# Mixer products in strips of the TensorE array: four strips of 32 columns, then four of 32 rows

## The chip, the core and the metric

The kernel runs on one core of a Trainium2 chip. Its engines work in parallel, each through its own list of instructions in order: TensorE (PE; its weight loads are listed as PEld), VectorE (DVE), ScalarE (ACT), GpSimd (POOL), and SyncE (SP), which here only issues DMAs. They wait for one another through semaphores. TensorE writes its products to PSUM, eight banks of 512 fp32 columns on 128 partitions; the other data lies in SBUF. The metric is the device time of one execution in microseconds.

## The reference

First attention with normalised queries and keys, over 8 batches, 12 heads, 448 positions and 64 dimensions a head; its output, the heads side by side, is a row of 768 for each position. Then a mixer over the positions, of rank 32, and an MLP.

```python
q_n, k_n = rmsnorm(q, g_q), rmsnorm(k, g_k)
attn = softmax(q_n @ k_n.T / 8)          # per batch and head: 448 x 448
x = (attn @ v)                           # per batch, heads side by side: 448 x 768
h = x.T @ U @ V                          # U: 448 x 32, V: 32 x 448
u = x + h.T
out = u + relu(u @ w_ch1) @ w_ch2        # 768 -> 3072 -> 768
```

## The kernel before

Positions are laid on the 128 partitions, three full blocks and a rest of 64, and two neighbouring batches share the block that holds their rests. `xs[b]` holds the attention output of batch b as `[128, 4, 768]` in bf16, `uT` the mixed rows turned (768 on the partitions in six tiles), which is what the first product of the MLP reads. Below, b counts from 0: batch 2 of the title is b = 1.

**The two lists.** After the attention of b = 0, the work stands in two lists. `att` holds the attention of the later batches: `Spair` (the scores of a pair of heads: two products into single banks of the pool `ps`, four into two double-bank tiles of the pool `ps_sc`, one more into `ps`, all but the last on 64 rows of the array, and five exponentials on ACT), `V` (14 products with the values, then a reciprocal and a multiplication on VectorE), and the preparation of the next queries and keys (squares on ACT, sums on VectorE, roots on ACT, scaling on GpSimd, `turn_dma` with four transposing DMAs on SP, `take_dma` with two multiplications on GpSimd). `mlp` holds `up` (six products of 448 columns and a relu), `down` (six products of 384 columns; four of these parts make a tile, which VectorE adds to u and SP stores), and the mixers of b = 1 to 7.

**The planner.** The loop that begins at line 884 takes from one list or the other. It carries `at`, its own estimate of when TensorE, ACT and VectorE will be free, from the costs that each step declares with `runs`; `due` says how far attention should be for a given progress of the MLP, and `ready` holds back scores where ACT or VectorE is late by these estimates. It fixes an order; on the chip each engine follows its own part of it.

**The pools.** `ps` has four banks, `ps_sc` two tiles of two banks, which together are all eight. A tile of a pool is given again when its last reader is done.

**The mixer of b = 1 to 7** is placed among the last steps of `down` of the batch before (line 770: 14 steps before their end for b = 1, 20 for the others):

- `mix_t` (line 480): the first product, x times U, turned. For each of six column tiles of x, four products with the x tile as weights and U, 32 columns, as the moving side: 24 products. VectorE copies the result, 128 x 192, into one of two buffers.
- `mix_tr` (line 491): two transposes on TensorE, which bring the rank onto the partitions (32 of them for each of four column tiles), and a copy on VectorE.
- `mix_rows` (line 530), eight times, for each of four blocks of rows and each half of 384 columns: three products with `Vm` as weights, 128 columns each. `Vm` holds V four times, each copy in its own 32 partitions with zeros in the others, so that a product over all 128 rows picks one column tile. VectorE adds x (line 546). After the second half SP issues one transposing DMA into `uT` (line 552), four a batch. The first `up` of the batch reads `uT` and needs all four.

One step of `down` stands between two of these parts. Where scores come in between, the parts are moved back by a step (lines 909 to 915). `turning` keeps loads back until the last part. The mixer of b = 0 uses another path (`mix_t0`, `mix` and `mix_rows` with `tz`), which stays.

Of the kernel before, what the change touches and what calls it, by code (L numbers as in the profile page):

```python
# [13 lines left out]
ALU = AluOpType  # L14
# [12 lines left out]
def kernel(  # L27
# [278 lines left out]

    NQ = P // rank
    Vf = outp.tile([P, dm], FP32, name="ob", tag="ob")[:, :S]
    Vm = consts.tile([P, NQ, S + R], BF16)

    nc.gpsimd.memset(Vm, 0.0)

    def prep_v(lo, hi):
        for m in range(lo, hi):
            r = slice(m * rank, (m + 1) * rank)
            cols = Vf[r].rearrange("r (p j) -> r j p", j=NT)
            nc.gpsimd.tensor_copy(Vm[r, m, :SM].rearrange("r (t i p) -> r i t p", i=2, t=NJ),
                                  cols[:, :2 * NJ].rearrange("r (i t) p -> r i t p", i=2))
            nc.gpsimd.tensor_copy(Vm[r, m, SM:S], cols[:, 2 * NJ])


    Uz = first[:, 0, :NW * P].rearrange("p (j r) -> p j r", r=P)
# [3 lines left out]
        nc.gpsimd.tensor_copy(Ub, Uf)  # L326
        nc.gpsimd.tensor_copy(Uz[:, :, :rank], Uf[:, :NW, :])

    tb_bufs = [consts.tile([P, 2 * P], BF16, name=f"tb{i}") for i in range(2)]

    def fill_mixer():
        nc.gpsimd.memset(Uz, 0.0)
        for t in tb_bufs:
            nc.gpsimd.memset(t, 0.0)


    at = {"pe": 0.0, "act": 0.0, "dve": 0.0}
# [2 lines left out]
    def runs(eng, us):  # L340
        at[eng] = us + (at["pe"] if eng == "pe" else max(at["pe"], at[eng]))
# [137 lines left out]

    def mix_t(b):  # L480

        pt = ps.tile([P, KD, rank], FP32, name="pu", tag="ps")
        for dt in range(KD):
            for j in range(NW):
                nc.tensor.matmul(pt[:, dt, :], xs[b][:, j, dt * P:(dt + 1) * P], Ub[:, j if j < NJ else NJ + b % 2, :],  # L485
                                 start=(j == 0), stop=(j == NW - 1))
        nc.vector.tensor_copy(tb_bufs[b % 2][:, :KD * rank], pt.rearrange("p k r -> p (k r)"))
        runs("pe", 0.62)
        runs("dve", 0.35)

    def mix_tr(b):
        pt = ps.tile([P, 2, P], BF16, name="pw", tag="ps")
        for i in range(2):
            nc.tensor.transpose(pt[:, i, :], tb_bufs[b % 2][:, i * P:(i + 1) * P], ident)
        tTs[b] = headp.tile([P, 2, P], BF16, name="tT", tag="tT")
        nc.vector.tensor_copy(tTs[b], pt)
        runs("pe", 0.11)
        runs("dve", 0.3)

    def mix_t0(lo, hi, scalar=False):  # L500

# [8 lines left out]
    def mix(b, dt, scalar=False):  # L510
        off = 64 if b % 2 == 0 else 0
        ph = ps.tile([P, S], FP32, name="ph", tag="ps")
        xb = xs[b][:, :, dt * P:(dt + 1) * P]
        nc.tensor.matmul(ph, tz[:, dt * P:(dt + 1) * P], Vm[:, 0, :S], start=True, stop=False)
# [15 lines left out]
    def mix_rows(b, w, half):  # L530

        odd = b % 2
        off = 0 if odd else 64
# [3 lines left out]
        if b < ROWS_FROM:  # L537
            nc.tensor.matmul(ph, Vm[:, 0, vc:vc + P], tz[:, h], start=True, stop=True)
        for i in range(HALF // P) if b >= ROWS_FROM else ():
            dt = half * (HALF // P) + i  # L540
            nc.tensor.matmul(ph[:, i * P:(i + 1) * P], Vm[:, dt % NQ, vc:vc + P], tTs[b][:, dt // NQ, :],  # L541
                             start=True, stop=True)
# [3 lines left out]
        nc.vector.tensor_tensor(dst, ph[lo:hi], x[lo:hi], ALU.add)  # L546
        runs("pe", 0.17)
        runs("dve", 0.56)
        if half == 1 and b >= ROWS_FROM:
            full = xs[b][:, w, :] if w < NJ else u_rest[lo:hi, :]  # L550
            c = off + w * P
            nc.sync.dma_start_transpose(uT[:, :, c:c + hi - lo], full)

    def up(b, ht):
        off = 64 if b % 2 == 0 else 0
# [92 lines left out]
    def turns(gi):  # L648
# [16 lines left out]
        (3, 1): [V2(2, 0)],  # L665
        (3, 2): turns(2),
        (3, 3): [V2(2, 1), (0, take_k, (2, 1)), (0, squares, (3, 0, pool)), (0, values, (2,)), (0, load, (5,)),
                 (0, weights, (1,)), (0, prep_v, (0, 1)), (0, squares, (3, 1, pool)), (0, weights, (1,))],
# [5 lines left out]
        (5, 3): [(0.39, mix, (0, 1)), (0.2, mix_t0, (512, 640)), (0, prep_v, (1, NQ)), (0, weights, (2,))],  # L674
    }
    for i in range(NPAIR):
        for r in range(4):
# [89 lines left out]
            done_at[a[0]] = n + 1 if a[0] > 0 else first_done  # L767


    PRE = (14, 20)  # L770
    mlp = []
    for b in range(B):
        for ht in range(KH):
# [5 lines left out]
        nb = b + 1  # L779
        pre = {}  # L780
        if ROWS_FROM <= nb < B:
            pre[n - PRE[nb > 1]] = [(0.77, mix_t, (nb,), nb)]
            pre[n - PRE[nb > 1] + 1] = [(0.11, mix_tr, (nb,), nb)]
            for piece in range(2 * NW):
                pre.setdefault(n - PRE[nb > 1] + 2 + (piece if nb > 1 else piece // 2), []).append(
                    (0.17, mix_rows, (nb, *divmod(piece, 2)), nb))
        tiles = [(col, half) for col in cols for half in range(2)]
        if b == 0:
            tiles.sort(key=lambda t: t[1])
# [73 lines left out]
        return a_two + (a_all - a_two) * (c - SECOND) / (m_end - m_one - SECOND)  # L863

    def mixes(f):
        return f in (mix_t, mix_tr, mix_rows)

    def ready(f, a):
        if f is Spair:
            if im > 0 and mixes(mlp[im - 1][1]):  # L870
                return False
            return at["dve"] <= at["pe"] + 0.3 and at["act"] <= at["pe"] + 1.0
        if f is V and ca >= a_one and (after_pair or after_v):
            return False
        if f is sums and a[0] > DMA_FROM:
            return not any(m[1] in (mix_t, mix_tr) for m in mlp[max(0, im - 1):im + 3])
        if ca >= a_one:
            return True
        if f is V:
            return exp_done[a[:2]] <= at["pe"] + 0.1  # L880
        return f is not Srows or at["act"] <= at["pe"] + 0.6

    later, turning, after_pair, after_v = [], False, False, False
    while ia < len(att) or im < len(mlp):
# [21 lines left out]
            if f is T and a == (DMA_FROM - 1, 1):  # L906
                nc.vector.memset(kp[:, 2 * NJ:], 0.0)
        else:
            if after_pair and mixes(mlp[im][1]):
                nb, n, moved = mlp[im][3], im, []  # L910
                while mixes(mlp[n][1]) and mlp[n][3] == nb:
                    e = next(i for i in range(n, len(mlp)) if mlp[i][1] is down)
                    moved += [mlp[e], *mlp[n:e]]
                    n = e + 1
                mlp[im:n] = moved
            after_pair = after_v = False
            c, f, a, _ = mlp[im]
            f(*a)
            turning = f is mix_t and a[0] > 0 or turning and a != (a[0], NW - 1, 1)
            cm += c  # L920
            im += 1

# [29 lines left out]
```

## Time and profile before

| | |
|---|---|
| median of 3 runs | 582.67 us (581.82 to 583.47) |
| profiled execution | 582.16 us, span 580.3 us |
| PE, PEld | 570.9 us (98%), 338.7 us (58%) |
| ACT | 308.2 us (53%) |
| POOL | 210.2 us (36%) |
| DVE | 196.3 us (34%) |
| granted TensorE clock | 1.00 |

The span is what the instructions of the core cover; the time also holds what lies around it. A product on TensorE is listed with its duration to the last result, but the next may start long before that, so the cost of a product in a stream is read from differences of starts, not from its own duration. A form such as 64*128 beside a product tells how many rows and columns of the array it uses.

### The profile page before, as it was taken

What the parts mean: (1) busy time and instruction counts of PE and PEld (TensorE: products, weight loads), DVE (VectorE), ACT (ScalarE), POOL (GpSimd) and SP (SyncE); (2) the same over time, 40 slices, a digit from 0 to 9 for tenths busy, and PEclk for the clock granted to TensorE, in tenths of its full rate; (3) what the DMA queues carried; (4) which work ended last, traced back from release to release, by engine and by line L of the source; (5) the groups of instructions that cost most, each with busy time, mean ns of one, the idle gap of its engine ahead of it and who ended that gap; (6) DMA issues with size and microseconds to landing.
All of it is one profiled execution on the core that took longest, in us unless ns stands there. A gap on an engine that the chain in (4) does not pass through costs nothing.

```text
span 580.3 us, 11778 instructions
## 1 busy us (share of the span) xinstructions
PE 570.9 (98%) x4850; PEld 338.7 (58%) x4850; DVE 196.3 (34%) x459; ACT 308.2 (53%) x510; POOL 210.2 (36%) x310
## 2 busy tenths in 40 slices
PE   8899999999999999999999999999999999999997
PEld 7655556555665556655566555665556555655565
DVE  5676656212353232521244230542034210410011
ACT  6866660787445776277635568357752444014300
POOL 5995684265314514334514532441531000000000
PEclk9999999999999999999999999999999999999999
DMA  9899999683547642765247745366204210330022
GB/s 235 168 241 241 244 232 223 128 209 73 135 79 170 156 106 35 175 179 130 36 123 116 179 104 122 80 159 150 36 16 102 49 28 1 54 76 1 1 55 55
DMA packets 104829, 68.21 MB, mean 118 GB/s; under 512 B 66632, under 2 KB 101704, under 8 KB 104776
## 3 DMA queue, kind: packets, MB, share of 16 engines
q1 hardware_dynamic: 95124, 57.83, 43.2%
q0 software_dynamic: 9408, 9.44, 9.7%
q8 instruction: 38, 0.62, 0.5%
q10 hardware_dynamic: 244, 0.20, 0.1%
q14 instruction: 15, 0.12, 0.1%
HBM read 52.20 MB, written 11.01 MB: 109 GB/s over the span
## 4 chain that ended last, share of the span: by engine, by line
PE 92%; ACT 2%; DMA 1%; POOL 1%; DVE 1%; issue 1%; SPq 0%; POOLq 0%; ACTq 0%
PE ph L558 36%; PE po L605 36%; PE pv L466 6%; PE sc L436 2%; PE pv L462 2%; PE sl L427 2%; PE sl L438 2%; PE pm L541 2%; PE po L592 1%; ACT E L416 1%; PE sc L415 1%; DMA qT<-qn 1%; PE pu L485 1%; DMA qf<-in_q_dram 1%; PE pt L354 1%
## 5 line engine op out<-in xcount | busy, mean ns | idle before, releaser
L605 PE MATMUL po<-w2b,hT 128*128 128x384 bf16 x1296 | 229.6, 326 | 0.0
L558 PE MATMUL ph<-uT,w1b 128*128 128x448 bf16 x1140 | 228.7, 352 | 0.0
L605 PEld LDWEIGHTS <-hT 128*128 128x128 bf16 x1296 | 122.1, 98 | 71.8
L558 PEld LDWEIGHTS <-w1b 128*128 128x128 bf16 x1140 | 108.3, 98 | 93.7 <-issue 0.7
L565 ACT ACTIVATE hT<-ph 128x448 bf16<-128x448 f32 x184 | 98.2, 551 | 116.6 <-PE ph L558 115.2
L429 ACT ACTIVATE E<-sl,gg 128x448 bf16<-128x448 f32 x72 | 41.6, 630 | 71.7 <-PE sl L427 71.7
L193 POOL TENSOR_TENSOR qn<-qf,rs 128x384 bf16<-128x384 f32 x36 | 29.9, 830 | 137.5 <-ACT rs L170 126.8
L386 POOL TENSOR_SCALAR qT<-qT,gg 128x448 bf16<-128x448 bf16 x36 | 50.5, 1403 | 73.6 <-DMA qT<-qn 63.5
L469 DVE RECIPROCAL r<-pv 128x4 f32<-128x4 f32 x96 | 17.5, 182 | 173.0 <-PE pv L466 172.8
L441 ACT ACTIVATE E<-sc,gg 128x896 bf16<-128x896 f32 x72 | 69.0, 1024 | 0.0
L615 DVE TENSOR_TENSOR ob<-po,x 128x384 f32<-128x384 f32 x46 | 25.7, 558 | 99.8 <-PE po L605 97.6
L466 PE MATMUL pv<-va,E 128*128 128x65 bf16 x1152 | 57.1, 194 | 0.0
L466 PEld LDWEIGHTS <-E 128*128 128x128 bf16 x1152 | 50.5, 98 | 6.3
L162 DVE TENSOR_REDUCE ssq<-sq 128x14 f32<-128x896 f32 x45 | 46.8, 1078 | 2.4 <-ACT sq L140 2.3
L462 PE MATMUL pv<-vl,E 128*128 128x130 bf16 x192 | 42.2, 220 | 0.3 <-ACT E L416 0.2
L470 DVE TENSOR_TENSOR x<-pv,r 128x256 bf16<-128x256 f32 x96 | 40.7, 424 | 3.3
L416 ACT ACTIVATE E<-sc,gg 128x896 bf16<-128x896 f32 (+1 forms) x42 | 37.5, 951 | 3.5 <-PE sc L415 3.3
L546 DVE TENSOR_TENSOR x<-pm,x 128x384 bf16<-128x384 f32 x48 | 26.1, 552 | 11.3 <-PE pm L541 9.1
L193 POOL TENSOR_TENSOR kp<-kf,rs 128x384 bf16<-128x384 f32 x36 | 29.9, 830 | 0.0
L169 ACT ACTIVATE rs<-ssq,eps 128x28 f32<-128x28 f32 (+1 forms) x25 | 7.9, 314 | 38.0 <-DVE ssq L162 33.7
L462 PEld LDWEIGHTS <-E 128*128 128x128 bf16 x192 | 18.7, 97 | 9.7 <-issue 2.0
L439 ACT ACTIVATE E<-sl,gg 128x448 bf16<-128x448 f32 x36 | 23.0, 638 | 0.0
(105 smaller groups left out, 401.0 us busy)
## 6 DMA issues: line engine op xcount, KB each, us to landing
qf<-in_q_dram SPq DMA_DIRECT2D x23, 448.0 KB, 3.8
kf<-in_k_dram SPq DMA_DIRECT2D x23, 448.0 KB, 5.3
vf<-in_v_dram SPq DMA_DIRECT2D x48, 192.0 KB, 5.3
out_dram<-ob SPq DMA_DIRECT2D x48, 192.0 KB, 2.8
w1b<-in_moe_w_ch_dram POOLq DMA_DIRECT2D x4, 1152.0 KB, 19.8
w2b<-in_moe_w_ch_dram POOLq DMA_DIRECT2D x8, 576.0 KB, 18.0
vf<-in_v_dram SPq DMA_DIRECT2D x48, 32.0 KB, 5.1
out_dram<-ob SPq DMA_DIRECT2D x13, 96.0 KB, 3.4
```

The lines of the kernel that those rows point to most:

```text
L162: nc.vector.tensor_reduce(ssqs[gi][:, i, :], sqs.pop((gi, i)), AX, ALU.add)
L193: nc.gpsimd.tensor_tensor(main.rearrange("p (t i) d -> p i t d", i=2), src[:, c, :2 * NJ].rearrange("p (i t) d -> p i t d", i=2), rs[:, c, ...
L386: nc.gpsimd.tensor_scalar(qT[:, a], qT[:, a], gg[:, 0:1], None, ALU.mult)
L416: nc.scalar.activation(es[(b, pr)][:, 2 * r:2 * r + n, :], sc[:, :n, :S], AF.Exp, scale=scal, bias=bias)
L429: nc.scalar.activation(E[:, 4 + i, :], ts[i], AF.Exp, scale=scal, bias=bias)
L441: nc.scalar.activation(E[:, 2 * r:2 * r + 2, :], tiles[r][:, :, :S], AF.Exp, scale=scal, bias=bias)
L462: nc.tensor.matmul(pv[:, i].rearrange("p e d -> p (e d)"), E[:, 2 * NJ, w:w + P], vl[:, lp, :], start=True, stop=False)
L466: nc.tensor.matmul(pv[:, i, e, :], E[:, 2 * j + e, w:w + P], va[:, (first_h + step * e) * NJ + j, :], start=False, stop=(e == 1 and j == N ...
L470: nc.vector.tensor_tensor(xs[b].rearrange("p i (h d) -> p i h d", d=D)[:, 2 * half:2 * half + 2, h0:h0 + step + 1:step, :], pv[:, :, :, :D ...
L558: nc.tensor.matmul(ph, w1b[:, dt, ht * P:(ht + 1) * P], uT[:, dt, off:off + S], start=(dt == 0), stop=(dt == KD - 1))
L565: nc.scalar.activation(hT[:, ht, off:off + S], ph, AF.Relu)
L605: nc.tensor.matmul(po, hT[:, ht, col:col + P], w2b[:, ht, half * HALF:(half + 1) * HALF], start=(ht == 0), stop=(ht == KH - 1))
```

## The change

The mixers of b = 1 to 7 use parts of the array.

- The first product takes U as the weights, 32 columns of the array, and x as the moving side, 192 columns. Four such products, one for each quarter of the 768 columns of x, go to four strips of 32 array columns and write four groups of 32 partitions of one bank. With four blocks of positions these are 16 products. The result has the rank on the partitions already, so the two transposes and their copy go.
- The second product takes 32 partitions of V as weights and the matching 32 partitions of the result as the moving side, on a strip of 32 array rows: for a block of rows, four products of 192 columns, one for each strip, into four different banks. `mix_two` does this for two blocks at once: eight products into both tiles of `ps_sc`, the banks that scores use, and then four additions on VectorE and two transposing DMAs. A mixer has two of them.
- `Vr`, V four times over the partitions without the zeros, takes the place of `Vm`; b = 0 reads it too, its other rows meeting zeros in `tz`. GpSimd fills and copies less.
- In the planner, `mix_two` stands 2 and 5 (b = 1) or 2 and 6 steps of `down` behind `mix_t`; where scores have just been placed, or ACT or VectorE is late by the planner's estimate, one step of `down` is taken first. `ready` and `turning` are fitted to the new names.

```diff
-    Vm = consts.tile([P, NQ, S + R], BF16)
-    nc.gpsimd.memset(Vm, 0.0)
-    def prep_v(lo, hi):
-        for m in range(lo, hi):
...
+    QC = dm // NQ
+    Vr = consts.tile([P, S + R], BF16)
+    nc.gpsimd.memset(Vr[:, S:], 0.0)
+    def prep_v():
+        cols = Vf.rearrange("r (p j) -> r j p", j=NT)
+        nc.gpsimd.tensor_copy(Vr[:, :SM].rearrange("r (t i p) -> r i t p", i=2, t=NJ),
+                              cols[:, :2 * NJ].rearrange("r (i t) p -> r i t p", i=2))
+        nc.gpsimd.tensor_copy(Vr[:, SM:S], cols[:, 2 * NJ])
...
     def mix_t(b):
-        pt = ps.tile([P, KD, rank], FP32, name="pu", tag="ps")
-        for dt in range(KD):
-            for j in range(NW):
-                nc.tensor.matmul(pt[:, dt, :], xs[b][:, j, dt * P:(dt + 1) * P], Ub[:, j if j < NJ else NJ + b % 2, :],
-                                 start=(j == 0), stop=(j == NW - 1))
-        nc.vector.tensor_copy(tb_bufs[b % 2][:, :KD * rank], pt.rearrange("p k r -> p (k r)"))
-        runs("pe", 0.62)
+        pt = ps.tile([P, QC], FP32, name="pu", tag="ps")
+        for j in range(NW):
+            for g in range(NQ):
+                nc.tensor.matmul(pt[g * rank:(g + 1) * rank, :], Ub[:, j if j < NJ else NJ + b % 2, :],
+                                 xs[b][:, j, g * QC:(g + 1) * QC], start=(j == 0), stop=(j == NW - 1))
+        tTs[b] = headp.tile([P, QC], BF16, name="tT", tag="tT")
+        nc.vector.tensor_copy(tTs[b], pt)
+        runs("pe", 0.6)
         runs("dve", 0.35)
-    def mix_tr(b):
...
+    def mix_two(b, ws):
+        odd = b % 2
+        off = 0 if odd else 64
+        ts = [ps_sc.tile([P, 2, 512], FP32, name="sc", tag="sc") for _ in range(2)]
+        for i, w in enumerate(ws):
+            vc = w * P if w < NJ else (SM if odd else S - P)
+            for g in range(NQ):
+                r = slice(g * rank, (g + 1) * rank)
+                nc.tensor.matmul(ts[g // 2][:, g % 2, i * QC:(i + 1) * QC], Vr[r, vc:vc + P], tTs[b][r], start=True, stop=True)
+        runs("pe", 0.4)
+        for i, w in enumerate(ws):
+            lo, hi = (0, P) if w < NJ else (0, R) if odd else (R, P)
+            full = xs[b][:, w, :] if w < NJ else u_rest[lo:hi, :]
+            for half in range(2):
+                h = slice(half * HALF, (half + 1) * HALF)
+                nc.vector.tensor_tensor(full[:, h].rearrange("p (g c) -> p g c", g=2),
+                                        ts[half][lo:hi, :, i * QC:(i + 1) * QC],
+                                        xs[b][lo:hi, w, h].rearrange("p (g c) -> p g c", g=2), ALU.add)
+                runs("dve", 0.56)
+            c = off + w * P
+            nc.sync.dma_start_transpose(uT[:, :, c:c + hi - lo], full)
...
-    PRE = (14, 20)
+    PRE, GAP = (14, 20), (5, 6)
...
-            pre[n - PRE[nb > 1]] = [(0.77, mix_t, (nb,), nb)]
-            pre[n - PRE[nb > 1] + 1] = [(0.11, mix_tr, (nb,), nb)]
-            for piece in range(2 * NW):
-                pre.setdefault(n - PRE[nb > 1] + 2 + (piece if nb > 1 else piece // 2), []).append(
-                    (0.17, mix_rows, (nb, *divmod(piece, 2)), nb))
+            at_ = n - PRE[nb > 1]
+            pre[at_] = [(0.6, mix_t, (nb,), nb)]
+            pre[at_ + 2] = [(0.4, mix_two, (nb, (0, 1)), nb)]
+            pre[at_ + GAP[nb > 1]] = [(0.4, mix_two, (nb, (2, 3)), nb)]
...
-            return not any(m[1] in (mix_t, mix_tr) for m in mlp[max(0, im - 1):im + 3])
+            return not any(m[1] is mix_t for m in mlp[max(0, im - 1):im + 3])
...
-            if after_pair and mixes(mlp[im][1]):
...
+            f = mlp[im][1]
+            if after_pair and mixes(f) or f is mix_two and max(at["act"], at["dve"]) > at["pe"]:
+                e = next((i for i in range(im, len(mlp)) if mlp[i][1] is down), None)
+                if e is not None and mlp[e][3] < mlp[im][3]:
+                    mlp.insert(im, mlp.pop(e))
...
-            turning = f is mix_t and a[0] > 0 or turning and a != (a[0], NW - 1, 1)
+            turning = f is mix_t or turning and not (f is mix_two and a[1][1] == NW - 1)
```

More of the change, by code (lines that the diff above doesn't have):

```diff
@@ L308 @@
     Vf = outp.tile([P, dm], FP32, name="ob", tag="ob")[:, :S]
-    Vm = consts.tile([P, NQ, S + R], BF16)
-    nc.gpsimd.memset(Vm, 0.0)
-    def prep_v(lo, hi):
-        for m in range(lo, hi):
[L315 to L319, printed above, removed]
+    QC = dm // NQ
+    assert NQ == 4 and 2 * QC <= 512 and HALF == 2 * QC
+    Vr = consts.tile([P, S + R], BF16)
[5 more added lines that the diff above has]
+        nc.gpsimd.tensor_copy(Vr[:, SM:S], cols[:, 2 * NJ])
     Uz = first[:, 0, :NW * P].rearrange("p (j r) -> p j r", r=P)
@@ L327, in prep_u @@
         nc.gpsimd.tensor_copy(Uz[:, :, :rank], Uf[:, :NW, :])
-    tb_bufs = [consts.tile([P, 2 * P], BF16, name=f"tb{i}") for i in range(2)]
     def fill_mixer():
         nc.gpsimd.memset(Uz, 0.0)
-        for t in tb_bufs:
-            nc.gpsimd.memset(t, 0.0)
     at = {"pe": 0.0, "act": 0.0, "dve": 0.0}
@@ L480, in mix_t @@
     def mix_t(b):
-        pt = ps.tile([P, KD, rank], FP32, name="pu", tag="ps")
-        for dt in range(KD):
-            for j in range(NW):
-                nc.tensor.matmul(pt[:, dt, :], xs[b][:, j, dt * P:(dt + 1) * P], Ub[:, j if j < NJ else NJ + b % 2, :],
-                                 start=(j == 0), stop=(j == NW - 1))
-        nc.vector.tensor_copy(tb_bufs[b % 2][:, :KD * rank], pt.rearrange("p k r -> p (k r)"))
-        runs("pe", 0.62)
-        runs("dve", 0.35)
-    def mix_tr(b):
[L492 to L498, printed above, removed]
+        pt = ps.tile([P, QC], FP32, name="pu", tag="ps")
@@ L513, in mix @@
         xb = xs[b][:, :, dt * P:(dt + 1) * P]
-        nc.tensor.matmul(ph, tz[:, dt * P:(dt + 1) * P], Vm[:, 0, :S], start=True, stop=False)
+        nc.tensor.matmul(ph, tz[:, dt * P:(dt + 1) * P], Vr[:, :S], start=True, stop=False)
         for j in range(NJ):
@@ L532, in mix_rows @@
         odd = b % 2
-        off = 0 if odd else 64
         h = slice(half * HALF, (half + 1) * HALF)
@@ L536, in mix_rows @@
         vc = w * P if w < NJ else (SM if odd else S - P)
[L537 to L542, printed above, removed]
+        nc.tensor.matmul(ph, Vr[:, vc:vc + P], tz[:, h], start=True, stop=True)
         x = xs[b][:, w, h]
@@ L548, in mix_rows @@
         runs("dve", 0.56)
[L549 to L552, printed above, removed]
     def up(b, ht):
@@ L667 @@
         (3, 3): [V2(2, 1), (0, take_k, (2, 1)), (0, squares, (3, 0, pool)), (0, values, (2,)), (0, load, (5,)),
-                 (0, weights, (1,)), (0, prep_v, (0, 1)), (0, squares, (3, 1, pool)), (0, weights, (1,))],
+                 (0, weights, (1,)), (0, prep_v, ()), (0, squares, (3, 1, pool)), (0, weights, (1,))],
         (4, 0): [V2(3, 0)],
@@ L673 @@
         (5, 2): [V2(4, 1), (0.39, mix, (0, 0))],
-        (5, 3): [(0.39, mix, (0, 1)), (0.2, mix_t0, (512, 640)), (0, prep_v, (1, NQ)), (0, weights, (2,))],
+        (5, 3): [(0.39, mix, (0, 1)), (0.2, mix_t0, (512, 640)), (0, weights, (2,))],
     }
@@ L865, in mixes @@
     def mixes(f):
-        return f in (mix_t, mix_tr, mix_rows)
+        return f in (mix_t, mix_two)
     def ready(f, a):
@@ L908 @@
         else:
-            if after_pair and mixes(mlp[im][1]):
[L910 to L915, printed above, removed]
+            f = mlp[im][1]
[3 more added lines that the diff above has]
+                    mlp.insert(im, mlp.pop(e))
             after_pair = after_v = False
```

## The prediction

> **What bounds the kernel now.** I read the page first (engines, chain), then a table of busy time in three stretches, then the timeline around one mixer (the mixing of a batch's rows through U and V) with no attention near it and around one with attention, and last the groups and DMA issues that the changed steps touch.
>
> The page's engines and its chain by engine, then the three stretches (busy us and instructions of each engine):
>
> ```profile
> PE 570.9 (98%) x4850; PEld 338.7 (58%) x4850; DVE 196.3 (34%) x459; ACT 308.2 (53%) x510; POOL 210.2 (36%) x310
> ...
> PE 92%; ACT 2%; DMA 1%; POOL 1%; DVE 1%; issue 1%; SPq 0%; POOLq 0%; ACTq 0%
> ```
>
> ```profile
> 0.00:45.00 45.00, 39.41 (x499) 28.85 (x500) 29.65 (x89) 32.45 (x50) 37.51 (x55) 1.00 0.97 215
> 45.00:465.00 420.00, 419.59 (x3614) 244.33 (x3613) 151.39 (x337) 249.73 (x413) 172.68 (x256) 1.00 0.59 130
> 465.00:580.00 115.00, 111.86 (x744) 65.48 (x740) 15.31 (x33) 26.00 (x48) 0.00 (x0) 1.00 0.16 34
> ```
>
> TensorE (PE) is busy 419.59 of the middle 420 us, at a granted clock of 1.00. All seven changed mixers lie after 45 us. There the time is the sum of what TensorE must issue: a microsecond off its list is a microsecond off the kernel, if no new wait appears.
>
> The mixer of batch 8 on TensorE (start, duration to the last result, line, count):
>
> ```profile
> 496.64 0.76 PE L485 MATMUL pu<-Ub,x 128*128 128x32 bf16 x24
> 497.25 1.14 PE L605 MATMUL po<-w2b,hT 128*128 128x384 bf16 x6
> 498.22 0.28 PE L494 MATMUL pw<-ident,tb 128*128 128x128 bf16 x2
> 498.33 1.14 PE L605 MATMUL po<-w2b,hT 128*128 128x384 bf16 x6
> 499.31 0.33 PE L541 MATMUL pm<-tT,Vm 128*128 128x128 bf16 x3
> 499.47 1.14 PE L605 MATMUL po<-w2b,hT 128*128 128x384 bf16 x6
> ```
>
> Differences of starts are the cost in the stream: 24 products of 32 columns take 0.61 us (25 ns each), two transposes 0.11, three products of 128 columns 0.16 to 0.17 (56 ns each), six of 384 columns 0.975 (163 ns each).
>
> Attention in the same stretch, all engines, rows left out:
>
> ```profile
> 225.04 1.14 PE L605 MATMUL po<-w2b,hT 128*128 128x384 bf16 x6
> ...
> 226.10 0.36 PE L427 MATMUL sl<-qT,kT 64*128 64x448 bf16 x2
> ...
> 226.30 0.54 PE L436 MATMUL sc<-qT,kT 64*128 64x448 bf16 x4
> ...
> 226.78 0.36 PE L438 MATMUL sl<-qT,kT 128*128 128x448 bf16 x1
> ...
> 226.98 1.14 PE L605 MATMUL po<-w2b,hT 128*128 128x384 bf16 x6
> ...
> 228.07 1.92 ACT L441 ACTIVATE E<-sc,gg 128x896 bf16<-128x896 f32 x2
> ```
>
> The 64*128 rows use half of the array's rows each; two of them together last 0.36 us, as long as one, so they run side by side. The whole set of scores takes 226.02 (225.04 + 0.975) to 226.98, 0.96 us, for four slots of 448 columns at 0.189 (six up products take 1.135) = 0.76. The other 0.20 is one change into the split array and back. The last exponential, which frees the score banks, ends at 229.99, 3.0 us after the scores.
>
> Groups and DMA issues that the changed steps touch:
>
> ```profile
> L546 DVE TENSOR_TENSOR x<-pm,x 128x384 bf16<-128x384 f32 x48 | 26.1, 552 | 11.3 <-PE pm L541 9.1 <-PE pm L538 2.2
> L496 DVE COPY tT<-pw 128x256 bf16<-128x256 bf16 x7 | 2.0, 292 | 9.1 <-PE pw L494 9.1
> ```
>
> ```profile
> uT<-x SPq DMA_TRANSPOSE x21, 2.8
> uT<-u_rest SPq DMA_TRANSPOSE x7, 2.4
> ```
>
> **The change part by part**, for one of seven batches.
>
> Removed from TensorE: 0.61 (first product) + 0.11 (transposes) + 8 x 0.167 = 1.33 (second product) = 2.05 us.
>
> Added, first product: 16 products of 192 columns in strips of 32 array columns. Between the 56 ns at 128 columns and the 163 at 384, 192 columns cost 83 ns. The trace has no strips of array columns. Ends: four strips side by side, 4 x 0.083 + 0.20 = 0.53; one after another, 16 x 0.083 + 0.20 = 1.52. I take side by side, since the 64*128 pairs are the nearest row, but with each weight load and product starting no closer than the 25 ns of the first product's row, the closest that any row shows for pairs of load and product in the full array: 16 x 0.025 + 0.20 = 0.60.
>
> Added, second product: twice eight products of 192 columns in strips of 32 rows. Ends: 2 x 0.083 + 0.20 = 0.37 each, or 8 x 0.083 + 0.20 = 0.86 each. By the same choice 8 x 0.025 + 0.20 = 0.40, together 0.80. The row tiling of the scores is the same mechanism with two strips, so I trust this more.
>
> Sum: 1.40 against 2.05, 0.65 a batch, 4.55 us in seven. Ends: 0.79 a batch (5.5 us) with all side by side at 83 ns a step, and a loss of 1.19 a batch (8.3 us) with nothing side by side.
>
> A rule speaks against the strips of columns. The Trainium skill (TensorE: Matmul & The Clock Gate, Part 3, "What overlaps and what doesn't") says that a weight load overlaps a running product only where their row groups differ; strips of columns share all rows. By that rule the first product would pay loads and products in turn. The trace disagrees for the whole array: 24 loads on the same rows last 96 ns each, yet start 25 ns apart; for strips of columns no run here shows it. By that rule the sum comes to the second price of the first rival below, 587.8; by the row, to 578.6.
>
> VectorE: the copy after the transposes (0.29 us) goes; the eight additions of 0.55 stay, now in two runs of four. The first copy stays at 0.36. VectorE is busy 36% of the middle stretch and hides this. GpSimd loses a 1.8 us fill, two of 0.3 and 3.5 us of copies of V, all before 45 us, where the chain to the first up products does not pass through them: nothing. SP issues the same four transposes a batch (1.2 us each), but in two bursts behind two runs of additions.
>
> New waits, by the order in the changed program. (a) A half mixer takes all four score banks, so it waits for the exponentials 3.0 us after the scores. In batches 3, 4 and 5 one half mixer stands exactly three steps of down (2.93 us) behind scores: 0.15 us each; the others stand further. TensorE runs in order, so everything behind waits too. (b) The next scores need the banks back from VectorE: from the half mixer's start 0.4 us to the first addition (before, a second product at 229.04 is followed by its addition at 229.41), 4 x 0.55, so 2.6, or 3.2 when a step's own addition is queued ahead. In batch 2 scores follow two steps of down later and reach the banks at about 2.7: 0.4 us. (c) Others that I can't place: some 0.1 us in each of the later batches. Taken together 1.0 us; bounds 0 and, from every half mixer waiting for one more pair of square activations that ACT has in front (0.97 each, 0.33 us a half on average), 4.6.
>
> Profiled execution 582.16 us (span 580.3 and 1.9 around it), less 4.55, plus 1.0: 578.6. It stood 0.5 below the median of the runs, 582.67, as near as these repeat.
>
> **The rivals.**
>
> Strips of columns one after another. For it: no row shows them working. Against: row strips do. Price: 1.52 instead of 0.60, 0.92 x 7 = 6.4 us, which gives 585.0; where loads are also not hidden (16 x 0.025 more a batch), 587.8. It decides as soon as the first product takes over 1.1 us.
>
> The banks eat the gain. For it: four banks, all taken, with ACT busy 59% of the middle stretch; against: most half mixers stand 3.4 us or more behind scores. With 4.6 us of waits the time is 582.2, no change.
>
> The transposes come late, and the first up product of each batch stalls: the mechanism that could make it slower with the products as cheap as I say. Place: the second half mixer's end. Before, eight additions came one by one over eight steps. Now the last additions end 2.6 to 3.2 us after the half mixer starts, the last transpose issues at 2.8 to 3.3 and lands 2.4 later (4.8 at the slowest of the 28): 5.2 to 8.1 us. Cover, from the order: 7.2 us in batch 3 (six steps of down 5.85, two value products 0.96, itself 0.40), 8 to 9.6 in batches 2 and 4 to 7, over 13 in batch 8. It costs from 7.2 on; if SP holds the transposes for 2 us more, behind the transposes of q and k that wait for GpSimd, six batches lose some 1.9 each: 11.4 us, 590.
>
> **How the numbers follow.** Strips side by side with small waits 0.66: 576.7 (5.5 saved, no wait) to 580.4. Gain eaten 0.13, around 582.2. Columns in turn 0.10, 585.0 to 587.8. Transposes late 0.11, around 590. A measurement here tells 0.3% (1.75 us) from no change: the first case is faster, the second the same, the last two slower. Range 576.5 to 585.0, which leaves out the late transposes and most of the columns in turn; the likeliest case's own range is 576.7 to 580.4.
>
> **What would show it.** Right: 16 first products with a form 128*32, four of them starting within 0.1 us, and the next down step 0.55 to 0.65 us after the first of them; eight second products in about 0.4; the middle stretch still nearly without gaps on TensorE. Wrong: starts 83 ns apart in the first product; a wait of TensorE on the exponential at the half mixers or on VectorE at the scores; a gap before the first up product of a batch that ends with the landing of a transpose.

## The result

The changed kernel takes 577.32 us (median of four executions, 577.21 to 579.24) against 582.32 us for the kernel before beside it: a ratio of 0.9919 with a 95% interval of 0.9906 to 0.9932, that is 4.7 us less by the ratio and 5.0 by the medians. A second set on another occasion gave 577.55 against 581.85, 0.9924 (0.9912 to 0.9937). The forecast was 578.6, with a range of 576.5 to 585.0. One execution of the runs below, the profiled one of the kernel with its first product on the whole array, fell into a slower state (600.56 us at a granted clock of 0.948, its nine others 583.1 to 584.5) and is left out.

The profiled execution took 577.21 us, with a span of 575.3 (before: 582.16 and 580.3).

### The profile page after: what moved, and what is told of

It reads as the page before. It is cut to its first block, busy times and chain, and to the rows that moved or that the text cites. A ratio compares the mean times of both kernels' runs of the same rounds, so it can differ in the third digit from the quotient of the medians.

```text
span 575.3 us, 11525 instructions
## 1 busy us (share of the span) xinstructions
PE 565.6 (98%) x4723; PEld 326.0 (57%) x4724; DVE 194.2 (34%) x452; ACT 307.3 (53%) x510; POOL 205.3 (36%) x302
## 4 chain that ended last, share of the span: by engine, by line
PE 93%; DMA 2%; ACT 2%; POOL 1%; issue 1%; DVE 1%; SPq 0%; POOLq 0%; ACTq 0%
PE ph L558 38%; PE po L605 36%; PE pv L461 6%; PE sc L431 2%; PE pv L457 2%; PE sl L422 2%; PE sl L433 2%; PE po L592 1%; DMA qf<-in_q_dram 1%; PE sc L410 1%; DMA vf<-in_v_dram 1%; ACT E L411 1%; PE sc L496 1%; PE pt L349 1%; POOL kp L174 1%
## 5 line engine op out<-in xcount | busy, mean ns | idle before, releaser
L605 PE MATMUL po<-w2b,hT 128*128 128x384 bf16 x1296 | 223.8, 326 | 0.0
L503 DVE TENSOR_TENSOR x<-sc,x 128x384 bf16<-128x384 f32 x42 | 20.8, 551 | 15.7 <-PE sc L496 15.7
L457 PEld LDWEIGHTS <-E 128*128 128x128 bf16 x192 | 18.7, 97 | 10.4 <-issue 2.7
```

Source lines behind the costliest of these rows:

```text
L457: nc.tensor.matmul(pv[:, i].rearrange("p e d -> p (e d)"), E[:, 2 * NJ, w:w + P], vl[:, lp, :], start=True, stop=False)
L605: nc.tensor.matmul(po, hT[:, ht, col:col + P], w2b[:, ht, half * HALF:(half + 1) * HALF], start=(ht == 0), stop=(ht == KH - 1))
```

## The profile after

The page's engines and its chain by engine:

```profile
PE 565.6 (98%) x4723; PEld 326.0 (57%) x4724; DVE 194.2 (34%) x452; ACT 307.3 (53%) x510; POOL 205.3 (36%) x302
...
PE 93%; DMA 2%; ACT 2%; POOL 1%; issue 1%; DVE 1%; SPq 0%; POOLq 0%; ACTq 0%
```

The three stretches (length, then busy us and instructions of PE, PEld, DVE, ACT, POOL, the granted clock, DMA share, GB/s):

```profile
0.00:45.00 45.00, 39.38 (x504) 28.76 (x506) 30.79 (x89) 32.55 (x51) 33.58 (x47) 1.00 0.98 216
45.00:465.00 420.00, 419.31 (x3540) 236.10 (x3538) 150.06 (x335) 250.23 (x415) 171.76 (x256) 1.00 0.61 131
465.00:575.00 110.00, 106.92 (x685) 61.19 (x682) 13.34 (x28) 24.49 (x45) 0.00 (x0) 1.00 0.15 32
```

TensorE is still busy all through the middle stretch (419.31 of 420, before 419.59) at a clock of 1.00, and still makes the chain. The time fell because its list is shorter: 565.6 us busy instead of 570.9.

The mixer of batch 8 in the timeline, where no attention is near (start, duration to the last result, line, form, count):

```profile
492.53 0.51 PE L480 MATMUL pu<-x,Ub 128*32 128x192 bf16 x16
492.98 2.12 PE L605 MATMUL po<-w2b,hT 128*128 128x384 bf16 x12
495.03 0.34 PE L496 MATMUL sc<-tT,Vr 32*128 32x192 bf16 x8
495.31 4.07 PE L605 MATMUL po<-w2b,hT 128*128 128x384 bf16 x24
499.31 0.34 PE L496 MATMUL sc<-tT,Vr 32*128 32x192 bf16 x8
499.59 5.70 PE L605 MATMUL po<-w2b,hT 128*128 128x384 bf16 x34
```

The form `128*32` is the strip of 32 columns, `32*128` the strip of 32 rows. Differences of starts hide a part here, because the change of form delays the first product itself: the last `down` product is followed by the first product after 256 to 259 ns instead of 162. With that included (from the start of the last product before, plus its own 162 ns, to the start of the next `down` product), the single records of the trace give this for seven batches:

| cost in TensorE's stream, us | before | after |
|---|---|---|
| first product | 4.23 | 3.78 (0.539 each) |
| transposes | 0.79 | none |
| second product | 9.41 | 5.30 (0.372 each, three of 14 at 0.404) |
| sum | 14.42 | 9.08 |

So 5.35 us left TensorE's list, 0.76 a batch. Inside a mixer, four products of the first kind start 1 to 5 ns apart, and the fours follow at 83, 72 and 73 ns; the `32*128` products do the same in two fours, 83 ns apart.

VectorE's additions and the transposes of the mixed rows (groups, and issues with the time to landing):

```profile
L503 DVE TENSOR_TENSOR x<-sc,x 128x384 bf16<-128x384 f32 x42 | 20.8, 551 | 15.7 <-PE sc L496 15.7
```

```profile
uT<-x SPq DMA_TRANSPOSE x21, 2.5
uT<-u_rest SPq DMA_TRANSPOSE x7, 2.5
```

They are as many as before (with the additions into the shared rest block and those of b = 0, which stand in other rows) and about as long: 0.55 us an addition, 2.5 us to landing, where the transposes of `x` took 2.8 before. Batch 2 is the one place where the change makes a new wait. TensorE there:

```profile
99.78 0.34 PE L496 MATMUL sc<-tT,Vr 32*128 32x192 bf16 x8
100.05 2.12 PE L605 MATMUL po<-w2b,hT 128*128 128x384 bf16 x12
102.11 0.36 PE L422 MATMUL sl<-qT,kT 64*128 64x448 bf16 x2
102.31 0.54 PE L431 MATMUL sc<-qT,kT 64*128 64x448 bf16 x4
102.78 0.36 PE L433 MATMUL sl<-qT,kT 128*128 128x448 bf16 x1
102.98 2.11 PE L605 MATMUL po<-w2b,hT 128*128 128x384 bf16 x12
105.03 0.36 PE L422 MATMUL sl<-qT,kT 64*128 64x448 bf16 x2
105.23 0.35 PE L431 MATMUL sc<-qT,kT 64*128 64x448 bf16 x2
106.04 0.37 PE L431 MATMUL sc<-qT,kT 64*128 64x448 bf16 x2 [0.46 <-ACT E L436]
```

The scores at 102.31, two steps of `down` behind the half mixer, waited for nothing. The next scores, only two steps behind these, waited for the exponentials of the set before: 0.81 us between two pairs that elsewhere stand 0.19 apart, so 0.62 lost. Before, those two sets stood four steps apart. Four microseconds on, at 110.12, the first `up` product of batch 2 waited 0.165 us for the last transpose.

The balance, from the first `up` product to the end of the last product: 535.72 us before, 531.18 after, 4.54 less. 5.35 came off in the mixers; 0.75 was given back at scores (0.62 in batch 2, 0.13 near 351 us, where pairs of scores start apart and no wait is recorded) and 0.165 at the first `up` of batch 2; the rest, 0.1, is spread over small waits that differ. The span shows 0.4 more gain because the work ahead of the first `up` ended at 40.74 instead of 41.14; the same work ended between 40.8 and 41.6 in the other runs that leave it as it is, so that part lies within the scatter.

## The experiments

The times to compare with are 577.3 for the changed kernel and 582.4 for the kernel before (582.43 and 582.37 beside these runs).

### Do the columns really run side by side?

Theory: four strips work at once, and within a strip one product follows the other. Rival: a strip is no unit at all; whatever 16 small products there are, they start as fast as they are issued. The first edit changes only the order of the list, so that four products of one strip follow each other.

```diff
-        for j in range(NW):
-            for g in range(NQ):
+        for g in range(NQ):
+            for j in range(NW):
```

> The same 16 first products in another order: the four blocks of positions of one strip of columns directly behind one another, then the next strip. Everything else, the order of all other work too, is as in the changed kernel. Theory (the gain of the first product is that four strips run side by side): products of one strip must follow one another at 83 ns, only the change of strip is at 4 ns, so the first product takes 0.09 + 12 x 0.083 + 0.01 + 0.18 = 1.28 us in place of 0.54, 0.74 more in each of seven batches, 5.2 us: 582.5, as long as the kernel before. Rival (fewer instructions and no transposes make the gain, the strips' overlap does not matter): 577.3, no change.

Measured: 577.99 us (577.33 to 578.77), ratio 0.9930 (0.9915 to 0.9945). The timeline at batch 8:

```profile
492.83 0.55 PE L480 MATMUL pu<-x,Ub 128*32 128x192 bf16 x16
493.31 0.99 PE L605 MATMUL po<-w2b,hT 128*128 128x384 bf16 x5
```

The 16 products take 0.48 us from the first start to the next `down`, against 0.45; with the change of form 0.570 against 0.539. My expectation of 5 us more was wrong. The starts now stand 13, 13, 14, 53, 13, 14, 13, 42 ns apart instead of 4, 3, 3, 83. So either a strip isn't busy for 83 ns, or the order of the list does not bind products that go to different strips. The next run tells these apart: nearly all products on one strip. It adds quarters of x together that do not belong together, so it leaves out the right result; the work has the same number and size.

```diff
+                s = g if j == NW - 1 else 0
-                nc.tensor.matmul(pt[g * rank:(g + 1) * rank, :], Ub[:, j if j < NJ else NJ + b % 2, :],
-                                 xs[b][:, j, g * QC:(g + 1) * QC], start=(j == 0), stop=(j == NW - 1))
+                nc.tensor.matmul(pt[s * rank:(s + 1) * rank, :], Ub[:, j if j < NJ else NJ + b % 2, :],
+                                 xs[b][:, j, g * QC:(g + 1) * QC], start=(s > 0 or j + g == 0), stop=(j == NW - 1))
```

> 13 of the 16 first products, those of the first three blocks of positions and one of the last, go to one strip of 32 columns and add into one region; the other three go to the other strips, so that every partition of the bank is written. Columns of different quarters of x are added together: this leaves out the right first product, the work is the same in number and size. If a strip takes one product at a time, 83 ns each: 13 x 0.083 + 0.27 = 1.35 us in place of 0.54, 0.8 more a batch, 5.7 us: 583.0. If what counts is only how many 32-column products run at once, whichever strip they name: no change, 577.4, and starts in groups of four 80 ns apart as before. The order of strips in the first experiment speaks for the second.

Measured: 582.44 us (582.22 to 583.70), ratio to the kernel before 1.0008 (0.9999 to 1.0018), so 5.1 us more than the changed kernel. Its timeline at batch 8:

```profile
493.00 4.06 PE L606 MATMUL po<-w2b,hT 128*128 128x384 bf16 x24
496.99 1.25 PE L481 MATMUL pu<-x,Ub 128*32 128x192 bf16 x16
498.17 2.12 PE L606 MATMUL po<-w2b,hT 128*128 128x384 bf16 x12
```

The 16 products last 1.18 us to the next `down` instead of 0.45; the 13 on one strip start 82 to 83 ns apart (the first pair 92), the three on the other strips 3 to 6 ns after one another. Cost in the stream 1.272 us, seven times 0.73 more: 5.1, all of the difference. A strip takes one product at a time, and the four work side by side. This run also shows that the order of the list does not bind products of different strips. The list ends with the three products of the other strips, and the last of them carries the semaphore that VectorE's copy waits for. In all seven mixers this record stands thirteenth of the 16 by its start, ahead of three older products of the long strip: at batch 8 it starts at 497.76, they start at 497.83, 497.91 and 497.99. The three records are also told by their duration, 0.257 us as for the first product on any strip, where the others last 0.246. The semaphore rises at 498.28, when all 16 have ended. This explains the first run: each strip gets its share at 83 ns a product, whatever the list says.

### What each half of the change is worth

The second product on all 128 rows, with a copy of V per 32 partitions and zeros elsewhere, as the kernel before had it; all else as changed:

```diff
+    Vm = consts.tile([P, NQ, S + R], BF16)
+    nc.gpsimd.memset(Vm, 0.0)
...
-                r = slice(g * rank, (g + 1) * rank)
-                nc.tensor.matmul(ts[g // 2][:, g % 2, i * QC:(i + 1) * QC], Vr[r, vc:vc + P], tTs[b][r], start=True, stop=True)
+                nc.tensor.matmul(ts[g // 2][:, g % 2, i * QC:(i + 1) * QC], Vm[:, g, vc:vc + P], tTs[b], start=True, stop=True)
```

> Only the strips of rows are undone: each second product runs over all 128 rows, with V's copy in 32 of them and zeros in the other 96, same 192 columns, same banks, same order. GpSimd fills and copies the zero-padded V again before 45 us. The result is the same. Theory (row strips side by side): eight products take 8 x 0.083 = 0.66 us without a change of the array's split, in place of 0.37, so 0.29 more in each of 14 half mixers, 4.1 us: 581.4. What is left against the kernel before, about 1 us, is then the first product's share. Rival (the order and the bursts make the gain): 577.3.

Measured: 581.49 us (580.95 to 582.65), ratio 0.9992 (0.9982 to 1.0001). Its timeline:

```profile
498.12 0.82 PE L503 MATMUL sc<-tT,Vm 128*128 128x192 bf16 x8
498.78 4.06 PE L612 MATMUL po<-w2b,hT 128*128 128x384 bf16 x24
```

Eight products on the whole array take 0.66 us, 83 ns each; on strips of rows 0.372 with the change of form. 14 times 0.288 is 4.0 us, and the time rose by 4.2. Then the first product on the whole array, with U padded to 128 columns in four copies:

```diff
+    Up = consts.tile([P, NJ + 2, NQ, P], BF16)
...
-                nc.tensor.matmul(pt[g * rank:(g + 1) * rank, :], Ub[:, j if j < NJ else NJ + b % 2, :],
-                                 xs[b][:, j, g * QC:(g + 1) * QC], start=(j == 0), stop=(j == NW - 1))
+                nc.tensor.matmul(pt, Up[:, j if j < NJ else NJ + b % 2, g, :], xs[b][:, j, g * QC:(g + 1) * QC],
+                                 start=(j == 0 and g == 0), stop=(j == NW - 1 and g == NQ - 1))
```

> Only the strips of columns are undone: each of the 16 first products uses the whole array, with U in 32 of 128 weight columns and zeros in the others, and all 16 add into one bank, which gives the same result. No change of the array's split around them; GpSimd prepares the padded U before 45 us; order of all other work as in the changed kernel. The order of products inside one strip made no difference (0.57 us in place of 0.54 with strips taken one by one), so that experiment did not undo the overlap; this one does. Theory (the gain of the first product is that four products share the array): 16 x 0.083 = 1.33 us in place of 0.54, 0.79 more in each of seven batches, 5.5 us: 582.8. Rival (overlap of products does not matter to the time): 577.3, or 1.3 us less without the changes of the split.

Measured: 583.4 us (583.1 to 584.5), ratio 1.0018 (1.0009 to 1.0028). That is 6.1 us more than with strips, 0.87 a batch, where 16 products at 83 ns less 0.539 would make 0.79; the rest is not traced. Without strips in either one of the two products, the gain over the kernel before is gone: 0.9 us is left in the first case, and the second is 1.1 us slower. This does not say what each half brings over the kernel before, since 16 products of 192 columns on the whole array (1.33 us) cost more than the old first product with its transposes (0.60 and 0.11). By the table above the first product brings 1.2 us (4.23 + 0.79 - 3.78) and the second 4.1 (9.41 - 5.30). No run has the new second product beside the old first one.

### What a change of form costs

One product on the whole array between the two blocks of a half mixer, which forces the form back and forth once more:

```diff
+            if i:
+                keep_busy(1)
```

> Between the four products of the first block and the four of the second in each half mixer stands one ordinary product of 128 columns on the whole array, whose result nobody reads. It forces one change of the array's split out and one back. Theory (a change out and back costs 0.19 us, 96 ns going in and 90 coming out, and the ordinary product 56 ns): 0.25 more in each of 14 half mixers, 3.4 us: 580.7; that is why two blocks share one visit. Rival (changes are nearly free, the 0.2 us belong to the products' own first weights): 14 x 0.056 = 0.8 us, 578.1.

Measured: 581.64 us (580.84 to 582.86), ratio 0.9990 (0.9980 to 0.9999). Its timeline:

```profile
498.12 0.26 PE L498 MATMUL sc<-tT,Vr 32*128 32x192 bf16 x4
498.32 0.23 PE L240 MATMUL busy<-ident 128*128 128x128 bf16 x1
498.48 0.26 PE L498 MATMUL sc<-tT,Vr 32*128 32x192 bf16 x4
498.68 4.07 PE L607 MATMUL po<-w2b,hT 128*128 128x384 bf16 x24
```

From the start of the first products to `down` it is 0.550 us instead of 0.276, behind the same entry: 0.274 more, of which the product itself is 0.056. One change out and back costs 0.22 us. Seven batches have three such changes each, 21 in all: some 4.6 us of the 9.08 that the mixers still take go to changes of form. The stream explains 14 times 0.274, 3.84 us, less the 0.165 at the first `up` of batch 2, which does not wait in this run: 3.67. The profiled executions stand 3.63 apart (580.84 and 577.21), the medians 4.3.

### What the wait rules in the planner are worth

The rule that holds a half mixer back by a step of `down` where ACT or VectorE is late was taken out; the rule for a mixer right behind scores stays.

```diff
-            if after_pair and mixes(f) or f is mix_two and max(at["act"], at["dve"]) > at["pe"]:
+            if after_pair and mixes(f):
```

> The planner's rule that takes a step of down ahead of a half mixer while ACT or VectorE is late is taken out; only directly behind scores one step of down still comes first. Five half mixers then stand one step of down, or one step and one value product, behind scores (1.1 to 1.5 us) instead of three or more. Theory (the half mixer takes all score banks and waits for the last exponential, 3.0 us after the scores): waits of 1.4 to 1.9 us on TensorE at these five, 8.2 us in all, 585.5. Rival (exponentials free the banks early enough, or the wait is absorbed by the next steps): 577.3.

Measured: 586.46 us (585.62 to 587.53), ratio 1.0074 (1.0056 to 1.0093): slower than the kernel before. Waits of TensorE (us in total, times, longest), and the timeline of one half mixer:

```profile
PE sc L496 <- ACT E L436: 6.8, 10, 1.0
```

```profile
227.57 1.14 PE L605 MATMUL po<-w2b,hT 128*128 128x384 bf16 x6
229.73 0.26 PE L496 MATMUL sc<-tT,Vr 32*128 32x192 bf16 x2 [1.02 <-ACT E L436]
230.62 0.34 PE L496 MATMUL sc<-tT,Vr 32*128 32x192 bf16 x6 [0.64 <-ACT E L436]
230.90 1.98 PE L605 MATMUL po<-w2b,hT 128*128 128x384 bf16 x6
```

Five of 14 half mixers stand one step of `down`, or a step and one `V` (14 products with the values), behind scores, and wait twice, once for each tile of `ps_sc`, until the exponentials have freed it: 1.5 to 2.0 us each, 8.4 in all. This is the rival "the banks eat the gain", with the price that it has where nothing keeps it away. In the changed kernel the same wait costs three times 0.03 us.

Six products of `down` after this wait last 1.98 us instead of 1.14. The stretch from 231 to 233 us (columns as above):

```profile
231.00:233.00 2.00, 2.00 (x11) 1.09 (x11) 1.98 (x5) 1.25 (x2) 0.00 (x0) 0.52 0.00 0
```

The granted clock is 0.52 there. It is 0.50 from 231.06 to 234.47: two waits of 1.1 and 0.9 us, with one pair of small products between them, cost another 1.7 us after they had ended, 0.8 of it at these six products (1.77 us, by starts, instead of 0.975). The like waits at 445.93 were followed by a clock of 1.00. Waits and clock come to 10.1 us, and the two waits of batch 2 do not occur here, 0.8 less; the time rose by 9.1.

### Where the transposes come late

The second half mixer was moved down the list, to 8 and 16 steps behind the first product:

```diff
-    PRE, GAP = (14, 20), (5, 6)
+    PRE, GAP = (14, 20), (8, 16)
```

> The second half mixer of each batch is placed about ten steps of down later, so that between its start and the first up product of the batch stand, by the order of the program, 4.7 us of work in batch 2, 3.8 in batch 3, 2.3 in batch 4, 0.4 in batches 5 and 6, 4.3 in batch 7 and 3.3 in batch 8, in place of 7 to 14. Theory (from the start of a half mixer to the landing of its last transpose 5.2 us must pass, 1.9 for four additions, then two issues of 1.3 and 2.4 to land): TensorE stands still for 1.4, 2.9, 4.8, 4.8, 0.9, 1.9 us and some 1 us in batch 2, 17 to 18 us in all: 595. Rival (the transposes are hidden anyway): 577.3.

Measured: 607.93 us (604.67 to 611.54), ratio 1.0445 (1.0400 to 1.0490). Waits of TensorE, and two stretches of 50 us:

```profile
PE ph L558 <- DMA uT<-u_rest: 16.0, 6, 4.9
```

```profile
300.00:350.00 50.00, 43.45 (x357) 23.91 (x354) 16.10 (x35) 20.30 (x35) 16.57 (x26) 0.90 0.56 119
400.00:450.00 50.00, 43.54 (x330) 23.16 (x328) 12.08 (x26) 29.97 (x53) 17.95 (x29) 0.93 0.38 90
```

The third rival has its mechanism here: the first `up` waits for the last transpose, 5.2 to 6.1 us from the half mixer's start, at the low end of the forecast chain of 5.2 to 8.1. In the changed kernel this `up` comes 7.15 us behind the half mixer in batch 3 and 8.1 to 13.9 in batches 4 to 8, so it waits in none of them. The run was 13 us slower than I expected. Its profiled execution took 604.67 us, 27.5 more than that of the changed kernel. In it the first `up` products wait 18.7 us, about the 17 to 18 that I expected; the rest has other causes. Two second half mixers now stand one step behind scores and wait for their banks, 4.0 us. And TensorE ran at a granted clock of 0.5 from 330.46 to 340.70 and from 405.56 to 412.38, which is why the two stretches show 0.90 and 0.93. What counts is the part of it behind the stalls, 5.8 and 4.0 us, in which the products take twice as long: 4.8 us lost by their starts. The other executions, up to 611.54 us at clocks of 0.978 to 0.983, left no trace.

The Trainium skill (TensorE: Matmul & The Clock Gate, Part 1, "What's actually happening") says that the array falls to half its clock after an idle window of about 3.4 us. In this trace the first fall comes 0.46 us into a stall of 4.9 us, directly behind two waits for the banks like those of the run above; the second comes 2.0 us into its stall, which also has two such waits ahead of it. Three stalls of 1.7 to 2.9 us without such waits left the clock at 1.00. So a stretch that isn't wholly idle can be enough; which stretch is, no run here settles. The stretches at half clock last 3.41, 10.24 and 6.83 us, one, three and two times 3.41, which agrees with the length of that window.

### Can the two waits of batch 2 be taken away?

First the scores: a set of scores not before three steps of the MLP have passed since the last.

```diff
-            if im > 0 and mixes(mlp[im - 1][1]):
+            if im > 0 and mixes(mlp[im - 1][1]) or since < 3:
```

> Scores may follow scores only after three steps of the MLP in place of two. It moves one set of scores in batch 2 back by one step of down; all else stays. In the changed kernel this set waits 0.62 us on TensorE for the exponentials of the set before, and the first up product of batch 2 another 0.165 for the landing of the last transpose. Theory (the transposes of batch 2 are held on SP by a store, and set the first up product): the 0.62 us go, the wait for the transpose grows to 0.6 to 0.8, and the time stays within 0.2 us: 577.2. Rival (the two waits are independent): 0.6 us less, 576.6, with the up product still 0.165 late.

Measured in one execution: 577.78 us, span 575.9. Its timeline around the first `up` of batch 2:

```profile
108.67 1.14 PE L605 MATMUL po<-w2b,hT 128*128 128x384 bf16 x6
110.70 1.29 PE L558 MATMUL ph<-uT,w1b 128*128 128x448 bf16 x6 [0.89 <-DMA uT<-u_rest]
```

The wait at the scores is gone and comes back at the `up` product, which stands 1.2 us behind its predecessor instead of 0.16. From the first `up` product to the end of the last product it is 531.39 us, against 531.18: no gain, as expected and against the rival. What sets this place is the transposes, which issue 2.3, 4.2, 6.7 and 8.1 us behind the half mixer. I thought that SP's order held them, behind loads and stores. So the second try also issues the first two of them from ScalarE's queue, which is idle there:

```diff
-            nc.sync.dma_start_transpose(uT[:, :, c:c + hi - lo], full)
+            q = nc.scalar if b == 1 and w < 2 else nc.sync
+            q.dma_start_transpose(uT[:, :, c:c + hi - lo], full)
```

> The change with two things mended, both in batch 2 only: scores follow other scores by at least three steps of the MLP (as in the run with the scores apart), and the transposes of the first two blocks of batch 2 are issued from ScalarE's queue, which is idle there (no activation from 90 to 102.5 us), instead of SP's, where they stood behind four loads and four stores. My theory: the wait of 0.62 us on the exponential goes, SP gets to the last two transposes at about +2 and +4 us behind the second half mixer instead of +6.5 and +7.8, and the first up product of batch 2 waits for nothing; 0.62 + 0.16 = 0.78 us less than the changed kernel: 576.5 where that takes 577.3. Rival: what holds the first up product is not SP's order but something else of the transposes (their own time to land, ScalarE's issue), so that it still waits 1 us and the time stays at 577.3 or above.

The changed kernel was run beside it:

> The changed kernel as it stands, on the same chip in the same rounds, for the comparison with the mended one: 577.3. Mended and unmended should differ by 0.8 us by my theory, by nothing by the rival.

Measured: 579.62 us (578.62 to 580.35), ratio 0.9962 (0.9949 to 0.9976), and for the changed kernel 577.55, 0.9924 (0.9912 to 0.9937). By the medians the mended one is 2.1 us slower than the unmended. The rival was right about the time, though not about the place: the first `up` waits for nothing here, and the time is lost ahead of it. The profiled executions (578.62, the fastest of five, and 577.82) show 0.8 of the difference; the rest has no trace. The timeline of the mended one:

```profile
96.13 1.95 DVE L503 TENSOR_TENSOR x<-sc,x 128x384 bf16<-128x384 f32 x4 [0.69 <-PE sc L496]
...
101.89 3.09 ACTq L509 DMA_TRANSPOSE uT<-x  x2
...
105.03 1.16 ACT L424 ACTIVATE E<-sl,gg 128x448 bf16<-128x448 f32 x2 [14.78 <-DMA out_dram<-ob]
...
105.72 2.11 PE L606 MATMUL po<-w2b,hT 128*128 128x384 bf16 x12 [1.33 <-ACT E L424]
...
107.30 1.27 SPq L509 DMA_TRANSPOSE uT<-x  x1
```

The additions that the first transposes read end at 98.08, and ScalarE's queue is empty, yet the first transpose issues at 101.89, when it did from SP too (101.81 to 102.05). Then both hold ScalarE's queue until 104.98, the exponentials behind them come 2.5 us late, TensorE waits 1.33 us for their bank, and the third transpose, on SP, issues only at 107.30, just after the second has landed at 107.15.

What holds them shows in the records of the DMA issues of the changed kernel (time of issue, semaphore that the DMA raises, time of landing where it was recorded; rows left out):

```
 92.70  qf load    109   99.35
 93.65  kf load    101  100.68
 94.15  vf load    102  -
 94.92  vf load    103  102.75
...
 99.46  ob store   109  105.34
100.70  ob store   101  105.70
101.81  uT<-x      102  -
103.67  uT<-x      103  106.53
```

Eight semaphores go round, and a DMA is not issued before the one that used its semaphore last has landed: the stores follow the landing of the loads eight issues earlier by 0.11 and 0.02 us. The first transpose, on 102, follows the last rise of its semaphore for the load, at 101.74, by 0.07, and in the mended run, from the other queue, by 0.06. The second has to wait only until the first one's issue ends, at 103.57. In the whole trace of the changed kernel all 311 issues that use a semaphore again stand behind its last rise for the DMA before. At most eight of these DMAs are under way, whichever queue issues them, and here the loads take 6 to 8 us to land. The first transpose of batch 2 therefore waits for the loads of the next queries, keys and values, and the others stand behind it. The round does not explain the third transpose of the mended run: its semaphore was free from 104.76. That it waited for the landing of the second, on the other queue, is read from the 0.15 us between them alone. A version with those loads placed elsewhere was not tried; by the two waits there are 0.8 us to be had.

## Why the prediction was right

The direction, the mechanism and the size hold. The sum came out 1.4 us above the profiled execution: 0.9 is the products that were priced too high, 0.4 the work ahead of the first `up`, which differs from run to run, 0.1 the rest. Step by step:

- **TensorE's list bounds the kernel.** Right: 5.35 us came off in the mixers, and 4.54 off the stretch that the list bounds.
- **First product, 0.60 a batch, chosen between 0.53 and 1.52.** Mis-sized by 0.06: it takes 0.539, at the low end. The limit of 25 ns for a pair of load and product, taken from the old product on the whole array, does not hold for strips, where pairs start 1 to 5 ns apart; what binds is 83 ns for each of four steps.
- **Second product, 0.40 each, between 0.37 and 0.86.** It takes 0.372, again the low end, for the same reason. Together with the first: 5.35 us saved instead of 4.55, and 5.45 but for the three short waits counted under (a).
- **The price of a split, 0.20,** read from the scores: 0.22 for a change out and back in the run that adds one, and 0.539 - 4 x 0.083 = 0.21, 0.372 - 2 x 0.083 = 0.21 in the mixers themselves. Right.
- **Waits, 1.0 us.** 0.1 for (a), the three half mixers that were named: each costs 0.03 more, not 0.15. (b) failed in its cause and hit the place: in batch 2 the first scores behind the half mixer did not wait for VectorE's additions, whose last ended at 102.09, 0.2 us before these products (2.3 us behind the start of the half mixer instead of the forecast 2.6 to 3.2, since four additions end 0.46 us apart); the second scores waited 0.62 us for exponentials, since the planner puts them two steps behind the first. (c), 0.1 in each later batch: 0.13 in one, near 351 us, nothing to be seen in the others. With the 0.165 at the first `up` of batch 2 they come to 1.0 as forecast, but by other waits: a sum that is right by chance.
- **The rule that spoke against the strips of columns** (the Trainium skill, TensorE: Matmul & The Clock Gate, Part 3, "What overlaps and what doesn't": a weight load overlaps a running product only where their row groups differ) does not hold here. All 16 loads use the same 128 rows and last 92 to 97 ns each, some 1.5 us in a row, yet the 16 pairs are done in 0.539 us. The row that the prediction set against it, 24 pairs 25 ns apart, was the better guide, and still too slow.
- **The rivals.** Columns one after another: fell, and the run with one strip shows what it would have cost, 5.1 us. Banks: kept away by the rule in the planner; without it 9.1 us. Transposes: they have 2 us of cover or more in batches 3 to 8 and none in batch 2, where 0.165 and 0.53 us were lost in two executions and nothing in four of the runs above. Moved late, they cost 18.7 us of the 27.5 that the profiled execution lost.

## What to carry to other kernels

Where TensorE's list is the bound and a product uses a quarter of the array's columns or rows, four strips give close to four times the rate (83 ns for four products of 192 columns), whatever the order of the list among the columns' strips, but each change of form costs 0.22 us out and back, so collect as many strip products as the banks hold behind one change. What the strips save is only kept if their banks are free: a half mixer one step behind the scores lost 1.5 to 2 us, five times or more what the strips save in it (0.29). And before moving a late DMA to another queue, see from the issue records what it waits for; here it was the landing of older DMAs, and the other queue only handed the wait to the exponentials.

## What was not expected

- Products of different strips of columns are not held by the order of the list: with four in a row on each strip the 16 take 0.570 us against 0.539 in the best order, and the last product of a list started ahead of three older ones.
- Stalls can cost more than their length: three times behind two waits of about 1 us, twice of these with a stall of 5 us following, TensorE ran at a granted clock of 0.5 for 3.4 to 10.2 us; once the same two waits left it at 1.00.
- No more than eight of these DMAs are under way at a time, since each waits for the landing of the one that used its semaphore before, on ScalarE's queue as on SP's.
